# Folding K and V in one strided sum, and dealing the setup steps by weight, in an attention + MoE + FFN kernel

## The chip, the cores and the metric

The kernel runs on one core of a Trainium2 chip. The metric is device time in microseconds (us) of one execution. Three runs of the kernel before took 1839.75, 1842.72 and 1853.4 us; the median is 1842.72 us.

## What is computed

Inputs are q, k, v of shape (8 batches, 8 heads, 576 tokens, 64), a gate, a noise and two expert weight sets, and two FFN weights. Cut to what matters here:

```
k_p = k.reshape(B, H, 72, 8, D).mean(axis=3)      # K and V pooled: 8 tokens become one
v_p = v.reshape(B, H, 72, 8, D).mean(axis=3)
attn = softmax(q @ k_p.T / sqrt(D)) @ v_p          # (8, 8, 576, 64)
x = attn.transpose(0, 2, 1, 3).reshape(4608, 512)
top2 of  x @ w_gate + log1p(exp(x @ w_noise)) * noise   -> 2 of 8 experts per token
out = sum over the two experts of weight * (relu(x @ w1[e]) @ w2[e])
h = out @ w_in;  result = (h * cos(h)) @ w_out
```

The change touches the first stage alone: the pooling of K and V, attention, gating, and the scatter of each token's row into the queues of its two experts.

## The kernel before, in words

**Stages.** Attention with gating takes about the first 290 us, then come the experts (about 290 to 1030 us) and the FFN. The experts start when all rows are scattered: `load_x` reads `xs` back, transposed, by DMA.

**Pairs, units, slots.** Attention works on pairs of batches, `g` = 0 to 3 (called pair 0 to pair 3). A tile is 128 tokens, 64 of each batch of the pair; a pair has R = 9 tiles. A *unit* is two tiles (the last unit of a pair has one), so a pair has 5 units and there are NU = 20, `u` = 0 to 19; `it = u % 5` is the place in the pair. A unit issues its work in the fixed order of the string `ORDER` (line 619): scores of unit u+2 (`S`, on TensorE, with a row maximum on VectorE), transposes of the exponentials of unit u (`T`), the softmax sums of unit u+1 (`N`, on VectorE, and a product on GpSimd, line 399), attention times V (`A`: matmuls into `xp`, a copy on ScalarE, a subtraction on VectorE), exponentials (`E`, ScalarE), transposes of q for unit u+3 (`Q`). Every engine runs its own instructions in the order of this program; the schedule is written out by hand (`manual_schedule`), and the framework only adds waits.

**Setup steps.** Beside the units there is work that belongs to another pair, cut into steps:
- `pooled` (lines 233 to 245): one chunk of K (`pk`, 5 steps) or of V (`pv`, 5 steps) of the next pair, folded on VectorE. A partition holds one window of 8 tokens x 64 for each of two batches, 1024 numbers; the step adds halves three times (512, 256 and 128 numbers; the last addition of K writes its 64 sums twice, side by side).
- `k_tr` (4 steps): three TensorE transposes and two ScalarE copies that put the pooled K into `kbd`, on partitions 0 to 63 and again on 64 to 127.
- `scale_v`, `scale_v2`, `v_tr` x 4, `g_proj1`, `g_proj2`: the scale of V, the seven GpSimd products that lay V out (`vbd`, line 292), its transposes, and the product of V with the gate weights.
- `gating` (10 steps `s1` to `s6` with two empty ones): logits, noise, top 2, ranks of the rows within their expert (`s5` is a group of matmuls, line 520, on what VectorE just wrote).
- `scatter` (9 steps, one per tile): two indirect DMAs each, issued by GpSimd (line 565).
- `prep_steps` for the first expert's weights, in pair 3 only (line 117).

**Slots.** `ORDER` has seven places `G` in a unit, called slots; at each, `go()` (line 621) issues the next steps of the list `fill`: their number over the slots left, rounded up. At the first unit of a pair the list is made: the setup of the next pair, mixed by count (`mix`) with the gating and the scatters of the pair before. In the last pair it is the weights of expert 0 mixed with gating and scatters of pair 2; its own gating follows in three parts in units 18, 19 and behind the loop (`CUTS`).

**Queues.** Loads are issued by the SyncE queue (SP) in program order; a load of K or V waits until its buffer (two of them, named `w1` in the code, `w` in the rows) has been folded. `zero_x` (one DMA) and `zero_y` (18) write zeros to DRAM from the same queue. GpSimd's queue (POOL) carries the softmax product of each unit, the layout of V and all scatters.

Of the kernel before, what the change touches and what calls it, by code (L numbers as in the profile page):

```python
# [34 lines left out]
def tile_attn_moe_ffn(ctx: ExitStack, tc: tile.TileContext, q, k, v, wgate, wnoise, noise,  # L35
# [192 lines left out]
    def setup_steps(g):  # L228
# [4 lines left out]
        def pooled(src, nm, i):  # L233
            def f():
                if i == 0:
                    X[nm + "f"] = src.pop(g).rearrange("p c b e -> p (c b) e")
                    X[nm] = ap_.tile([128, 10, 2 if nm == "ks" else 1, D], F32, name=nm)
                t, o = X[nm + "f"], X[nm]
                n = 64 if nm == "ks" and i == 4 else 128
                t, o = t[0:n, 2 * i:2 * i + 2, :], o[0:n, 2 * i:2 * i + 2, :, :]  # L240
                for w in (256, 128):
                    V.tensor_add(t[:, :, 0:w], t[:, :, 0:w], t[:, :, w:2 * w])  # L242
                dup = [n, 2, 2 if nm == "ks" else 1, D]
                V.tensor_add(o, t[:, :, None, 0:D].to_broadcast(dup), t[:, :, None, D:2 * D].to_broadcast(dup))
# [12 lines left out]
        def k_tr(b, half):
            def f():
                t = tr_half(X["ks"].rearrange("p c s d -> p c (s d)"), b, half).rearrange("p (h n) -> p h n", n=KP)
                for i in range(2):  # L260
                    A.activation(kbd[64 * i:64 * i + 64, b, 4 * half:4 * half + 4, i, :], t[64 * i:64 * i + 64],
                                 AF.Copy, scale=1.0 / 64.0)
            return f

        def scale_v():
            vp = X["vp"].rearrange("p c s d -> p c (s d)")
            m1 = ap_.tile([128, 1], F32, name="vm1")
            V.reduce_max(m1, vp, axis=AX.XY, apply_absolute_value=True)
            mb_ = ap_.tile([128, 128], F32, name="vmb")
            V.tensor_copy(mb_, m1.to_broadcast([128, 128]))  # L270
            X["mb"] = mb_

        def scale_v2():
            mb_, vp = X["mb"], X["vp"].rearrange("p c s d -> p c (s d)")
# [12 lines left out]
            vbd, vbd4 = GS[g]  # L287
            vp4 = vp.rearrange("p (c b) d -> p c b d", b=2)
            for c, o, i0, i1 in ((0, 64, 0, 2), (1, 0, 0, 1), (1, 80, 1, 3), (2, 0, 0, 3), (3, 0, 0, 1), (3, 80, 2, 3),
                                 (3, 144, 1, 2)):  # L290
                n = i1 - i0
                PL.tensor_mul(vbd[:, c, :, o:o + 64 * n].rearrange("p b (i d) -> p b i d", d=D),
                              vp4[:, c, :, None, :].to_broadcast([128, 2, n, D]),
                              rms[:, c, None, i0:i1, None].to_broadcast([128, 2, n, D]))
            V.tensor_scalar(vbd4[:, :, 16:80], vp[:, 8:10, :], s, None, op0=OP.mult)
            VBD[g] = GS[g]

        def v_tr(b, half):
            def f():
                if b == 0 and half == 0:  # L300
                    X["vt"] = ap_.tile([64, 2, S], F32, name="vtt")
                t = tr_half(X["vp"].rearrange("p c s d -> p c (s d)"), b, half)
                A.activation(X["vt"][:, b, 288 * half:288 * half + 288], t, AF.Copy)
            return f

# [311 lines left out]
    CUTS = {3: (0, 6), 4: (6, 8)}  # L617
    left = [0]
    ORDER = "S0 G T0 G T1 S1 E0 T2 N A0 G A1 E1 S2 G A2 Q0 E2 G S3 G A3 Q1 G E3".split()

    def go():
        k_ = -(-len(fill) // left[0])
        left[0] = max(left[0] - 1, 1)
        for f in fill[:k_]:
            f()
        del fill[:k_]

    for u in range(NU):
        g, r, n = UNITS[u]
        it = u % 5  # L630
        if it == 0:
            a = []
            if g + 1 < G:
                pk, kt_, pv, sv = setup_steps(g + 1)
                a = pk + pv[:2]
                for i in range(4):
                    a += kt_[i:i + 1] + pv[i + 2:i + 3]
                a += sv
                if g + 2 < G:
                    a.append(lambda g=g: (load_kv(g + 2, 0), load_kv(g + 2, 1)))  # L640
            if g == G - 1:
                p1, p2 = prep_steps(0, "w1"), prep_steps(0, "w2")
                p1.pop(0)()
                a = p1
            fill += mix(a, late)
            late = []
        if g == G - 1 and it in CUTS:
            r0, r1 = CUTS[it]
            gt = gating(g, r0, r1)
            gt.pop(0)()  # L650
            fill += gt + [scatter(g, r_) for r_ in range(r0, r1)]
            if it == 3:
                p2.pop(0)()
        left[0] = ORDER.count("G") * ((5 if g < G - 1 or it > 2 else 3) - it)
        if g == G - 1 and it == 3:
            left[0] = 6
        for op in ORDER:
            k_ = int(op[1:] or 0)
            if op == "A0":
# [16 lines left out]
                q_tr(u + 3, k_)  # L676
        if u == 2:
            zero_x()
        if 4 <= u <= 12:
            zero_y(2 * u - 8)  # L680
            zero_y(2 * u - 7)
        if it == 4:
            assert not fill
            if g + 2 < G:
                load_q(g + 2)
            if g < G - 1:
                late = gating(g, 0, R)
# [708 lines left out]
```

## Time and profile before

| what | value |
|---|---|
| median of three runs | 1842.72 us (1839.75 to 1853.4) |
| profiled execution, span from first to last instruction | 1814.0 us, 28.7 us below the median; the page gives no time beside the span |
| TensorE busy | 1721.6 us, 95% |
| VectorE, ScalarE, GpSimd busy | 1061.6, 928.8, 423.0 us |
[...]
| chain that ended last | TensorE 87%, VectorE 8%, ScalarE 2%, DMA 1%, GpSimd 1% |

The busy shares are means over very different stages: the FFN and the experts keep TensorE at 90% or more of nearly every slice, the first 315 us do not. So the attention stage has to be read by itself, in stretches of one pair and less. Pair 0 runs to about 97 us, pair 1 to 159, pair 2 to 220, pair 3 to about 282, and the first expert matmul starts at 301.5 us.

### The profile page before, as it was taken

How to read it: one execution, taken by the hardware profiler on the slowest of the kernel's cores; microseconds unless marked ns; L12 is line 12 of the kernel's file. 1: busy time of each engine (PE TensorE's matmuls, PEld its weight loads, DVE VectorE, ACT ScalarE, POOL GpSimd, SP SyncE). 2: the span in 40 equal slices, each digit the busy share in tenths (PEclk: the TensorE clock that was granted, in tenths of full speed). 3: DMA queues.
4: the chain of work that ended last, by engine and by line, in shares of the span. 5: the costliest groups of instructions: out<-in, count | busy, mean ns of one | idle time of the engine just before them, and what ended most of it. 6: DMA issues, size and time to landing. Idle time of an engine off the chain costs nothing.

```text
span 1814.0 us, 28287 instructions
## 1 busy us (share of the span) xinstructions
PE 1721.6 (95%) x11160; PEld 1017.4 (56%) x11160; DVE 1061.6 (59%) x2016; ACT 928.8 (51%) x1843; POOL 423.0 (23%) x457
## 2 busy tenths in 40 slices
PE   5977975999999999999999998999999999999999
PEld 3655652464445544464445545666666666666665
DVE  7787684644666484527674144666656566565633
ACT  4766851323233243323333235777777777767765
POOL 1225663000100000001110013524434243333222
PEclk8988986999999999999999999999999999999999
DMA  9978446456453738474744443313223031222100
GB/s 277 316 249 324 152 163 186 143 177 198 128 169 116 186 99 259 128 213 109 224 123 112 180 145 122 88 35 76 65 70 78 34 88 50 73 61 63 42 24 24
DMA packets 233206, 243.48 MB, mean 134 GB/s; under 512 B 154352, under 2 KB 167664, under 8 KB 232432
## 3 DMA queue, kind: packets, MB, share of 16 engines
q1 hardware_dynamic: 210544, 183.97, 35.0%
q0 software_dynamic: 11520, 37.76, 6.3%
q10 hardware_dynamic: 11008, 19.93, 3.1%
q8 instruction: 88, 1.44, 0.3%
q14 instruction: 46, 0.38, 0.1%
HBM read 127.06 MB, written 78.12 MB: 113 GB/s over the span
## 4 chain that ended last, share of the span: by engine, by line
PE 87%; DVE 8%; ACT 2%; issue 1%; DMA 1%; POOL 1%; SPq 0%; ACTq 0%; POOLq 0%; DVEq 0%
PE ph L1289 20%; PE ph L807 20%; PE py L832 19%; PE py L1252 15%; PE xp L450 3%; PE pt L1252 3%; PE sc L369 2%; DVE w L242 1%; PE py L847 1%; PE tr L416 1%; PE tr L353 1%; PE sc L254 1%; DVE amw L137 1%; DVE w L154 1%; ACT w L153 0%
## 5 line engine op out<-in xcount | busy, mean ns | idle before, releaser
L807 PE MATMUL ph<-xt,w 128*128 128x512 f16 (+1 forms) x2304 | 410.9, 336 | 11.1 <-DMA xt<-xs 11.1
L1289 PE MATMUL ph<-w,ht 128*128 128x512 f16 x1728 | 413.1, 379 | 1.0 <-POOL ht L1279 1.0
L832 PE MATMUL py<-w,ht 128*128 128x512 f16 x1728 | 384.4, 379 | 0.1
L807 PEld LDWEIGHTS <-w 128*128 128x128 f16 x2304 | 214.9, 98 | 198.0 <-issue 16.8
L1279 POOL TENSOR_TENSOR ht<-ty,ht 128x512 f16<-128x512 f32 x144 | 183.7, 1281 | 479.5 <-ACT ht L1278 323.8
L832 PEld LDWEIGHTS <-ht 128*128 128x128 f16 x1728 | 168.6, 98 | 199.1 <-DVE ht L820 0.6
L820 DVE SCALAR_TENSOR_TENSOR ht<-ph,ht 128x512 f16<-128x512 f32 (+2 forms) x192 | 109.9, 574 | 270.3 <-ACT ht L819 270.1
L1289 PEld LDWEIGHTS <-ht 128*128 128x128 f16 x1728 | 169.1, 98 | 152.8 <-POOL ht L1279 1.5
L1252 PEld LDWEIGHTS <-st 128*128 128x128 f16 x1872 | 183.1, 98 | 54.9 <-issue 4.0
L819 ACT ACTIVATE ht<-ph 128x512 f16<-128x512 f32 (+2 forms) x192 | 96.3, 502 | 184.4 <-PE ph L807 157.7
L835 ACT ACTIVATE yt<-py,ysc 128x512 f32<-128x512 f32 x72 | 49.4, 686 | 227.4 <-PE py L832 226.7
L1252 PE MATMUL py<-xt,st 128*128 128x256 f16 x1040 | 139.3, 273 | 3.5 <-ACT ht L1342 3.5
L1264 DVE SCALAR_TENSOR_TENSOR ty<-ty,k,ht 128x512 f32<-128x512 f32 x108 | 94.0, 871 | 83.1 <-ACT ty L1258 83.1
L1273 DVE SCALAR_TENSOR_TENSOR ty<-ty,ht 128x512 f32<-128x512 f32 x108 | 74.7, 692 | 108.8 <-ACT ty L1270 108.8
L1252 PEld LDWEIGHTS <-w 128*128 128x128 f16 x1152 | 112.7, 98 | 39.1 <-issue 3.8
L1269 ACT ACTIVATE ty<-ty,k 128x512 f32<-128x512 f32 x144 | 102.8, 714 | 22.9 <-DVE ty L1264 22.8
L1258 ACT ACTIVATE ty<-ht,k 128x512 f32<-128x512 f32 x108 | 77.4, 717 | 67.3 <-DVE ht L1343 34.1
L1252 PE MATMUL py<-w,st 128*128 128x256 f16 x832 | 111.7, 273 | 0.0
L1278 ACT ACTIVATE ht<-ty 128x512 f16<-128x512 f32 x144 | 89.5, 622 | 34.9 <-DVE ty L1273 34.3
L898 POOL TENSOR_TENSOR tm<-yg 128x512 f32<-128x512 f32 x32 | 33.8, 1057 | 302.7 <-DVE x L908 151.9
L1036 POOL DMA_INDIRECT yg<-yb,yidx x72 | 73.1, 1015 | 113.3 <-DMA yb<-yt 93.5
L1270 ACT ACTIVATE ty<-ty 128x512 f32<-128x512 f32 x144 | 90.7, 630 | 4.6
(249 smaller groups left out, 2095.2 us busy)
## 6 DMA issues: line engine op xcount, KB each, us to landing
yb<-yt ACTq DMA_DIRECT2D x72, 256.0 KB, 3.2
st<-in_moe_w_dram SPq DMA_DIRECT2D x8, 2048.0 KB, 13.5
yg<-in_moe_w_in_dram SPq DMA_DIRECT2D x32, 512.0 KB, 4.9
yg<-in_moe_w_out_dram SPq DMA_DIRECT2D x32, 512.0 KB, 4.4
yb<-zt SPq DMA_DIRECT2D x18, 768.0 KB, 19.8
st<-in_moe_w_dram SPq DMA_DIRECT2D x8, 1536.0 KB, 7.7
w<-in_k_dram SPq DMA_DIRECT2D x16, 512.0 KB, 5.8
w<-in_v_dram SPq DMA_DIRECT2D x16, 512.0 KB, 8.8
```

Source lines behind the costliest of these rows:

```text
L807: PE.matmul(ps[:, 0:n], w[:, a_, k_, 128 * f:128 * f + 128], xt[:, 4 * b_ + k_, 0:n], start=(i == 0), stop=(i == 11))
L819: A.activation(t[:, 0], p, AF.Relu)
L820: V.scalar_tensor_tensor(t[:, 1], p, 0.0, t[:, 0], op0=OP.max, op1=OP.subtract)
L832: PE.matmul(ps[0:m], ht[:, a_, f, 128 * t:128 * t + m], w[:, b_, f, :], start=(i == 0), stop=(i == 23))
L1252: PE.matmul(o, FW["in"][4 * a_ + 2 * sa + k_][:, f:f + 128], x[:, :, sb, k_, :], start=(start and h == 0 and k_ == 0 and j == 0), stop=(k_ ...
L1258: A.activation(y, h, AF.Identity, bias=CB["k4", c][:, 0:1])
L1264: V.scalar_tensor_tensor(y, y, CB["k4", c][:, 0:1], h, op0=OP.subtract, op1=OP.subtract)
L1269: A.activation(y, y, AF.Sin, scale=CB["k4", c][:, 1:2])
L1270: A.activation(y, y, AF.Square, scale=math.sqrt(2.0 * CC))
L1278: A.activation(g[:, 2 * b, :], y, AF.Copy)
L1279: PL.tensor_sub(g[:, 2 * b + 1, :], y, g[:, 2 * b, :])
L1289: PE.matmul(ps, g[:, 2 * b + a_, 256 * h + 128 * tt:256 * h + 128 * tt + 128], FW["out"][b_][:, k_, :], start=(q_ == 0 and b < 2 and h == ...
```

## The change

Four things, all in the attention stage:
1. `pooled` is one `reduce_sum` over the 8 tokens of a window: 1024 numbers in, 128 out, the 8 numbers of one sum 64 apart (256 bytes). K's sums are stored once.
2. Because K's sums are stored once, its transposes give 64 partitions, and both copies into `kbd` read partitions 0 to 63.
3. The steps carry weights. A pair's steps fall into two lists: units 0 to 2 take K (and the gating of the pair before), units 3 and 4 take V (and the scatters of the pair before, which had followed the gating). `blend` merges two lists by weight; `go()` issues steps while half the next weight still fits into the mean weight per slot.
4. K and V of the pair after next are loaded right behind their own folds, no longer behind all of the setup; `zero_y` comes two units later.

```diff
         def pooled(src, nm, i):
...
-                for w in (256, 128):
-                    V.tensor_add(t[:, :, 0:w], t[:, :, 0:w], t[:, :, w:2 * w])
-                dup = [n, 2, 2 if nm == "ks" else 1, D]
-                V.tensor_add(o, t[:, :, None, 0:D].to_broadcast(dup), t[:, :, None, D:2 * D].to_broadcast(dup))
+                t = X[nm + "f"][0:n, i]
+                V.reduce_sum(X[nm][0:n, 2 * i:2 * i + 2, :], t.rearrange("p b (r d) -> p b d r", d=D), axis=AX.X)
...
-                    A.activation(kbd[64 * i:64 * i + 64, b, 4 * half:4 * half + 4, i, :], t[64 * i:64 * i + 64],
+                    A.activation(kbd[64 * i:64 * i + 64, b, 4 * half:4 * half + 4, i, :], t,
...
+    def gate_steps(gt):
+        return cost(gt, 0.3, 0.6, 0.6, 1.4, 1.5, *[0.3] * (len(gt) - 9), 0.5, 0.3, 1.0, 0.7)
     def go():
-        k_ = -(-len(fill) // left[0])
-        left[0] = max(left[0] - 1, 1)
-        for f in fill[:k_]:
-            f()
-        del fill[:k_]
+        goal = sum(c for c, _ in fill) / max(left[0], 1)
+        last = left[0] <= 1
+        left[0] -= 1
+        done = 0.0
+        while fill and (last or done + fill[0][0] / 2 <= goal):
+            done += fill[0][0]
+            fill.pop(0)[1]()
...
+        if it == 0 and g + 1 < G:
+            pk, kt_, pv, sv = setup_steps(g + 1)
+            a = cost(pk, 1.2)
+            if g + 2 < G:
+                a.append((0.0, lambda g=g: load_kv(g + 2, 0)))
+            fill += blend(a + cost(kt_, 0.4), gate_steps(late))
+            late = cost([scatter(g - 1, r_) for r_ in range(R)] if g else [], 0.3)
+            left[0] = 3 * NG
+        elif it == 3 and g + 1 < G:
+            a = cost(pv, 1.2)
+            if g + 2 < G:
+                a.append((0.0, lambda g=g: load_kv(g + 2, 1)))
+            fill += blend(a + cost(sv, 1.2, 0.0, 2.5, 0.4), late)
+            left[0] = 2 * NG
+        elif it == 0:
+            p1, p2 = prep_steps(0, "w1"), prep_steps(0, "w2")
+            p1.pop(0)()
+            fill += blend(cost(p1, 1.2, 1.2, 1.2, 1.2, 1.5, 1.3),
+                          gate_steps(late) + cost([scatter(g - 1, r_) for r_ in range(R)], 0.3))
+            left[0] = 3 * NG
+        elif g == G - 1 and it in CUTS:
...
+            fill += gate_steps(gt) + cost([scatter(g, r_) for r_ in range(r0, r1)], 0.3)
+            left[0] = NG
...
-        if 4 <= u <= 12:
-            zero_y(2 * u - 8)
-            zero_y(2 * u - 7)
+        if 6 <= u <= 14:
+            zero_y(2 * u - 12)
+            zero_y(2 * u - 11)
```

Carrying out the two rules by hand gives the steps of each slot (a bar between slots, "-" an empty one; K0 is the first fold of K, am and sp the maxima and splits of expert 0's weights, sc a scatter):

```
pair 1 before, unit 0  K0 s1 | K1 s2 | K2 s3 | K3 s4a | K4 V0 | s4b V1 | nop kt0
               unit 1  s5 V2 | kt1 nop | V3 | s5b | kt2 | s6 | V4
               unit 2  kt3 | sc0 | scv | sc1 | nop | sc2 | scv2
               unit 3  vt0 | sc3 | vt1 | sc4 | vt2 | sc5 | vt3
               unit 4  gp1 | sc6 | nop | sc7 | gp2 | sc8 | load
pair 1 after,  unit 0  K0 | s1 s2 | s3 | K1 | - | - | s4a
               unit 1  K2 | - | - | s4b | K3 | nop | K4
               unit 2  s5 | nop | s5b | loadK kt0 | kt1 kt2 | s6 | kt3
               unit 3  V0 | sc0 V1 | sc1 V2 | sc2 V3 | sc3 V4 | sc4 loadV | scv
               unit 4  sc5 nop | - | - | scv2 | sc6 vt0 sc7 vt1 | vt2 vt3 sc8 | gp1 nop gp2
pair 0 after: the five K folds in unit 1 slot 3 to unit 2 slot 4, the five V folds in slots 1 to 5 of unit 3
pair 3 before, unit 15 am0 s1 | s2 s3 | am1 s4a | s4b am2 | nop s5 | am3 nop | s5b scl
               unit 16 s6 | sc0 | sp0 | sc1 | sc2 | sp1 | sc3
               unit 17 sc4 | sp2 | sc5 | sc6 | sp3 | sc7 | sc8
pair 3 after,  unit 15 am0 | s1 s2 | s3 | am1 | s4a | am2 | s4b
               unit 16 am3 | scl | nop s5 | nop | sp0 | s5b | s6
               unit 17 sp1 | sc0 sc1 | sp2 | sc2 sc3 sc4 | sc5 | sp3 | sc6 sc7 sc8
```

## Rows read from the trace of the kernel before

**Rows 1.** Page, slices of 45 us: busy tenths of TensorE.
```profile
PE   5977975999999999999999998999999999999999
```
**Rows 2.** Busy time by stretch (columns: stretch, length, engines' busy us, PEclk, DMA, GB/s).
```profile
62.00:97.00 35.00, 34.83 (x384) 25.27 (x385) 23.24 (x71) 29.95 (x112) 10.92 (x11) 1.00 1.05 318
97.00:120.00 23.00, 13.30 (x124) 8.95 (x124) 21.79 (x62) 10.71 (x40) 2.12 (x1) 0.77 0.95 349
120.00:135.00 15.00, 14.64 (x162) 10.51 (x162) 12.30 (x36) 12.03 (x46) 4.74 (x6) 0.90 0.29 89
135.00:159.00 24.00, 23.36 (x249) 16.91 (x246) 13.55 (x46) 20.33 (x76) 21.37 (x36) 1.00 1.03 359
220.00:267.00 47.00, 34.77 (x348) 24.45 (x348) 37.74 (x113) 28.00 (x98) 30.19 (x47) 0.85 0.44 158
```
**Rows 3.** Waits, 97 to 135 us (who for whom: us, times, longest).
```profile
PE tr L520 <- DVE g_ohb L514: 6.1, 1, 6.1
```
**Rows 4.** Groups by line, VectorE and ScalarE, 97 to 135 us (busy us, mean ns).
```profile
L242 DVE TENSOR_TENSOR w<-w 128x512 f32<-128x512 f32 (+3 forms) x20 | 13.9, 696 | 0.3
L244 DVE TENSOR_TENSOR ks<-w 128x256 f32<-128x256 f32 (+1 forms) x5 | 2.1, 424 | 0.2
L244 DVE TENSOR_TENSOR vp<-w 128x128 f32<-128x128 f32 x5 | 1.5, 292 | 0.2
L261 ACT ACTIVATE kbd<-sc 64x288 f32<-64x288 f32 x8 | 3.2, 406 | 0.2 <-PE sc L254 0.2
```
**Rows 5.** Groups by line and shape, VectorE reductions, 0 to 400 us.
```profile
L137 DVE TENSOR_REDUCE amw<-st 128x1 f32<-128x1024 f32 x16 | 19.2, 1208 | 0.0
...
L923 DVE TENSOR_REDUCE fm<-yg 128x1 f32<-128x512 f32 x10 | 6.8, 675 | 0.0
...
L533 DVE TENSOR_REDUCE g_osum<-g_ohb 128x8 f32<-128x72 bf16 x3 | 0.8, 272 | 0.0
```
**Rows 6.** The same view, 267 to 301 us: line 533 on 48 numbers.
```profile
L533 DVE TENSOR_REDUCE g_osum<-g_ohb 128x8 f32<-128x48 bf16 x1 | 0.2, 232 | 0.0
```
**Rows 7.** Timeline of VectorE (start us, duration us, instruction).
```profile
29.82 3.05 DVE L242 TENSOR_TENSOR w<-w 128x512 f32<-128x512 f32 x2
...
97.09 1.14 DVE L242 TENSOR_TENSOR w<-w 128x512 f32<-128x512 f32 x2
...
103.17 3.02 DVE L242 TENSOR_TENSOR w<-w 128x512 f32<-128x512 f32 x2
...
226.99 1.21 DVE L137 TENSOR_REDUCE amw<-st 128x1 f32<-128x1024 f32 x1
```
**Rows 8.** Timeline of GpSimd: softmax products beside them, and scatters of pairs 2, 3.
```profile
103.06 2.12 POOL L399 TENSOR_TENSOR ex<-ex,rc 128x1152 f32<-128x1152 f32 x1 [6.93 <-DVE rc L398]
...
226.87 2.11 POOL L399 TENSOR_TENSOR ex<-ex,rc 128x1152 f32<-128x1152 f32 x1 [1.50 <-PE sc L369]
...
237.79 1.01 POOL L565 DMA_INDIRECT xs<-xr,idx  x1 [8.78 <-DVE mb L112]
...
288.82 0.96 POOL L565 DMA_INDIRECT xs<-xr,idx  x1 [0.22 <-issue]
```
**Rows 9.** Chain that ended last, in order of time: start, us, what.
```profile
8.81 0.61 DVE w L242
10.32 0.61 DVE w L242
...
290.08 4.47 DMA xs<-xr,idx
```
**Rows 10.** VectorE's softmax sums of units 16 and 17 (timeline).
```profile
240.53 1.04 DVE L394 TENSOR_REDUCE sm<-ex 128x12 f32<-128x864 f32 x1
...
252.89 1.04 DVE L394 TENSOR_REDUCE sm<-ex 128x12 f32<-128x864 f32 x1
```
**Rows 11.** SyncE's queue: load of K of pair 2.
```profile
56.69 8.40 SPq L77 DMA_DIRECT2D w<-in_k_dram  x5
```
**Rows 12.** DMA issues 60 to 100 us: KB each, median us to landing.
```profile
w<-in_k_dram SPq DMA_DIRECT2D x2, 512.0 KB, 14.8
```

More of the change, by code (lines that the diff above doesn't have):

```diff
@@ L235, in f @@
                 if i == 0:
-                    X[nm + "f"] = src.pop(g).rearrange("p c b e -> p (c b) e")
-                    X[nm] = ap_.tile([128, 10, 2 if nm == "ks" else 1, D], F32, name=nm)
-                t, o = X[nm + "f"], X[nm]
+                    X[nm + "f"] = src.pop(g)
+                    X[nm] = ap_.tile([128, 10, D], F32, name=nm)
                 n = 64 if nm == "ks" and i == 4 else 128
-                t, o = t[0:n, 2 * i:2 * i + 2, :], o[0:n, 2 * i:2 * i + 2, :, :]
-                for w in (256, 128):
-                    V.tensor_add(t[:, :, 0:w], t[:, :, 0:w], t[:, :, w:2 * w])
-                dup = [n, 2, 2 if nm == "ks" else 1, D]
-                V.tensor_add(o, t[:, :, None, 0:D].to_broadcast(dup), t[:, :, None, D:2 * D].to_broadcast(dup))
+                t = X[nm + "f"][0:n, i]
+                V.reduce_sum(X[nm][0:n, 2 * i:2 * i + 2, :], t.rearrange("p b (r d) -> p b d r", d=D), axis=AX.X)
             return f
@@ L265, in scale_v @@
         def scale_v():
-            vp = X["vp"].rearrange("p c s d -> p c (s d)")
+            vp = X["vp"]
             m1 = ap_.tile([128, 1], F32, name="vm1")
@@ L301, in f @@
                     X["vt"] = ap_.tile([64, 2, S], F32, name="vtt")
-                t = tr_half(X["vp"].rearrange("p c s d -> p c (s d)"), b, half)
+                t = tr_half(X["vp"], b, half)
                 A.activation(X["vt"][:, b, 288 * half:288 * half + 288], t, AF.Copy)
@@ L619, in tile_attn_moe_ffn, with cost, blend @@
     ORDER = "S0 G T0 G T1 S1 E0 T2 N A0 G A1 E1 S2 G A2 Q0 E2 G S3 G A3 Q1 G E3".split()
-    def go():
-        k_ = -(-len(fill) // left[0])
-        left[0] = max(left[0] - 1, 1)
-        for f in fill[:k_]:
-            f()
-        del fill[:k_]
+    NG = ORDER.count("G")
+    def cost(fs, *w):
+        return [(w[min(i, len(w) - 1)], f) for i, f in enumerate(fs)]
+    def blend(a, b):
+        sa, sb = sum(c for c, _ in a) + 1e-9, sum(c for c, _ in b) + 1e-9
+        out, i, j, ca, cb = [], 0, 0, 0.0, 0.0
+        while i < len(a) or j < len(b):
+            if j >= len(b) or (i < len(a) and ca * sb <= cb * sa):
+                ca += a[i][0]
+                out.append(a[i])
+                i += 1
+            else:
+                cb += b[j][0]
+                out.append(b[j])
+                j += 1
+        return out
+    def gate_steps(gt):
+        return cost(gt, 0.3, 0.6, 0.6, 1.4, 1.5, *[0.3] * (len(gt) - 9), 0.5, 0.3, 1.0, 0.7)
+    def go():
+        goal = sum(c for c, _ in fill) / max(left[0], 1)
[5 more added lines that the diff above has]
+            fill.pop(0)[1]()
     for u in range(NU):
@@ L630, in tile_attn_moe_ffn @@
         it = u % 5
[L631 to L647, printed above, removed]
+        if it == 0 and g + 1 < G:
[7 more added lines that the diff above has]
+        elif it == 3 and g + 1 < G:
+            assert not fill
+            a = cost(pv, 1.2)
[10 more added lines that the diff above has]
+        elif g == G - 1 and it in CUTS:
             r0, r1 = CUTS[it]
@@ L688, in tile_attn_moe_ffn @@
                 late.pop(0)()
-                late += [scatter(g, r_) for r_ in range(R)]
     tabs = const.tile([1, 3, OVT], I32, name="tabs")
```

13 lines of the change are left out of this document (4 added, 9 removed).

## The prediction

> **What bounds the kernel now.** The page first: TensorE is busy in nine tenths or more of nearly every slice of 45 us, but in six of the first seven it is not [rows 1]. So I read that part by stretch. From 62 to 97 us TensorE works 34.83 of 35.00 us at full clock and VectorE idles 12 us: TensorE is the bound there. From 97 to 120 us, the opening of pair 1, VectorE works 21.79 of 23.00 us and TensorE 13.30, at a mean granted clock of 0.77. From 135 to 159 us TensorE is the bound again and VectorE idles 10.4 us [rows 2]. The waits name the place: TensorE stands 6.1 us before the rank matmuls of `s5`, for what VectorE writes in `s4` [rows 3]; VectorE is late because all ten folds fall into this stretch, 13.9 + 2.1 + 1.5 = 17.5 us of its work [rows 4]. Pair 2 opens the same way. So a pair loses about 10 us to uneven dealing, twice; the limit of any gain is some 20 us of 1842.72. After attention nothing changes: experts and FFN keep their time.
>
> The profiled execution has a span of 1814.0 us and the page knows no time beside it; the median run is 28.7 us longer. I add the changes to the span and carry the 28.7 along.
>
> **The fold.** Now a fold of K takes 1.51 us from start to start (10.32 - 8.81) [rows 9]; one of V ends with 292 ns in place of 424 [rows 4], so 1.38. A fold that meets the GpSimd product of a softmax is stretched: its first two additions took 3.02 us in place of 1.14, while the product ran [rows 7, 8]. The new step is a reduction of 1024 numbers, 64 apart, which no row shows. From below: line 137 reduces 1024 adjacent numbers in 1.208 us. A step of two numbers costs nothing visible: 512 of them take 0.675 us, about what half of line 137 plus its fixed part gives. But line 533 reads its 72 numbers eight apart (16 bytes) and takes 272 ns [rows 5], and 232 ns for 48 [rows 6]: 1.67 ns each, against 1.04 in line 137 and 923 (1208 - 675 over 512). By that slope the fold takes 0.152 + 1024 x 0.00167 = 1.86 us. I take it, since a step of 256 bytes is nearer to one of 16 bytes than to none. Upper end: that, stretched by 0.6 us on average, which is a third of the 1.9 us that the product added to the additions: 2.5 us. I don't take the stretch, since the reduction of line 137 ran through a product undisturbed, 1.21 us from 226.99 while the product ran from 226.87 to 228.98 [rows 7, 8]. Consecutive instructions overlap by some 0.08 us, so a fold occupies 1.78 us (ends: 1.13 and 2.4).
>
> [...]
>
> **The sum.**
> 1. Start: the five K folds of pair 0 lie on the chain [rows 9]: 5 x (1.78 - 1.51) = **+1.3** (ends -2, +4.5). Its V folds: 5 x 0.4 more, less the 1.9 us of the one that collided at 29.82 [rows 7]: **0** (-2, +3).
> 2. Pair 0, unit 0: K's folds leave it, **-1** (0 to -2): TensorE works there almost without a break.
> 3. Units 0 to 2 of pairs 1 and 2 (38 us in pair 1): VectorE has 21.79 + 12.30 = 34.1 us; without ten folds and with five new ones 34.1 - 17.5 + 8.9 = 25.5. TensorE has 13.30 + 14.64 = 27.9, less at full clock. If nothing collided, 28.5 us; with the ratio of the weight stretch of pair 3, where VectorE works 37.74 of 47.00 us and TensorE 34.77 [rows 2], 25.5 x 1.245 = 31.7. I take 31: units 0 and 1 hold more VectorE than TensorE work and unit 2 less. **-7** each.
> 4. Units 3 and 4 of pairs 0, 1, 2: five V folds come into slots 1 to 5 of unit 3. For two units VectorE has 13.55 - 0.7 + 8.9 = 21.8 us against TensorE's 23.36 of 24.00 [rows 2], but unit 3 alone gets about 14 us of it (an estimate: its own 4, 8.9 of folds, 1.1 of `scv`), where a unit at TensorE's pace lasts about 9.2 us (62 to 97 us holds some 3.8 units). Three PSUM buffers each for scores and products let TensorE run ahead by part of a unit. The last three slots hold all four V transposes and both gate products; their ScalarE copies meet a ScalarE that is busy 29.95 of 35.00 us. I take **+2** for each of the three pairs (0 to +5).
> 5. Pair 3: the weights and gating come more evenly, so units 15 and 16 end 4 us earlier (half of TensorE's waits there). But the scatters of pair 2 start in unit 17, not 16, 12.4 us later by the sums of these units [rows 10] if nothing else moved. GpSimd issues two per tile, 1.26 us apart [rows 8], 36 in all, and softmax products of 2.1 us between: 45.4 + 2.1 = 47.5 us from the first. Now it starts at 237.79 and the last issue starts at 290.08 [rows 8, 9], some 5 us of it idle. Starting at 237.8 + 12.4 - 4 = 246.2, it ends at about 293.7 against 291: **+3** (0 to +8).
>
> Without cost, and why: `kbd` gets its second copy from partitions 0 to 63, 406 ns now [rows 4]; a copy across partitions is not shown, I take the same; twice that would be 3.2 us a pair on ScalarE in slots with spare time, 1 us of it seen. The transposes of K get narrower, a gain below 0.5 us. K's last copy sits in the last slot ahead of the scores that need it: under 1 us, within term 3. Scatters of pairs 0 and 1 in units 3 and 4: 18 x 1.26 = 22.7 us of GpSimd with V's layout and two products, about 29 us in 20, so GpSimd is late by a few us, and the product of the next unit waits behind it; now it is as full, 21.37 of 24 us [rows 2], and TensorE is not late. SP: K of pair 2 is issued at 56.69 now [rows 11], and then only when pair 0's unit 2 has folded K, near 78; it lands some 15 us later [rows 12], just ahead of its first fold near 96; `zero_x` and `zero_y` queue behind it, and nothing needs them soon. If K came late, VectorE would stand once, for 2 or 3 us.
>
> Sum: +1.3 + 0 - 1 - 14 + 6 + 3 = -4.7. **Span 1809, time 1838 us**: a gain that a measurement can hardly tell, since less than 1% (18 us) is not told from no change.
>
> **Rivals.**
> - *Fold at the rate of adjacent numbers*, 1.21 us (1.13 occupied), as line 137. For it: line 923; against it: line 533. Start -4, pair 0 -1 + 1, units 0 to 2 at TensorE's 28.5 us, -9.5 each, units 3 and 4 of pairs 1 and 2 +0.5 each, pair 3 +3: -19, **1824 us**.
> - *The fold is the bound, and it is slower*: 2.5 us. Place: the open slots of units 0, 1 and 3. VectorE then has 34.1 - 17.5 + 12 = 28.6 us in units 0 to 2, 35.6 with the ratio above, -2.4 each; unit 3 holds 17 us in place of some 10, +6 in each pair; start +7.5; pair 0 unit 1 +1; pair 3 +3: -4.8 + 18 + 11.5 = +25, **1867 us**. It turns from gain to loss where a fold takes about 2 us. For it: 40 folds now stand whole in the queue; against it: the slope of line 533. [...]
> - *GpSimd bounds the end*: units 15 and 16 gain nothing, so the scatters end 7 to 8 us later, and the bunches at the ends of units 3 and 4 cost their upper ends: -4.7 + 4 + 6 = +5, **1848 us**. For it: GpSimd's issues follow each other without a break to 291 us.
>
> **Numbers.** Forecast 0.46 (its own range 1829 to 1848), first rival 0.30, second 0.12, third 0.12. The range 1817 to 1856 leaves out the lower tail of the first rival and most of the second. Faster by over 1% (below 1824): half of the first rival and a little, 0.17. Slower by over 1% (above 1861): most of the second, 0.10. Within: 0.73.
>
> **What would show it.** In the trace after: the mean of the one reduction in place of lines 242 and 244 (1.8 to 1.95 us; 1.2 is the first rival, 2.4 the second), also under GpSimd's products; TensorE's wait for `s4` below 2 us; pair 1 from about 96 to 151 us with the clock near 1; a wait of TensorE in unit 3 of each pair; first scatter of pair 2 near 245 us and a start of the experts 3 us later in relation to unit 15. Wrong would make it above all the fold's price, then a VectorE that is late at unit 3 by more than the PSUM buffers take up.

## The result: slower by 1.4%, and the profile after

The changed kernel takes 1867.86 us (median of four runs, 1866.85 to 1872.22), the kernel before beside it 1844.24: a ratio of 1.0139, 95% interval 1.0101 to 1.0178. I had forecast 1838 and given slower by over 1% one chance in ten.

The page of the changed kernel: its profiled execution took 1866.85 us, 1.75 more than its span.

```profile
span 1865.1 us, 28210 instructions
...
PE 1735.2 (93%) x11160; PEld 1022.5 (55%) x11160; DVE 1074.8 (58%) x1936; ACT 927.3 (50%) x1843; POOL 423.2 (23%) x457
...
PE   5887774599999999999999999999999999999999
```

Against [rows 1] the gap of TensorE is a slice longer; the first expert matmul starts at 352.99 us, and from there to the end both kernels take the same, 1512.1 and 1512.5 us. All of the difference lies in attention.

**One trap first.** The trace that I predicted from cannot be set against this one as it stands. The kernel before takes 1836 to 1853 us in some sets of runs (chips 0, 2 and 15) and 1814 to 1818 in others (chips 5 and 6); all runs of one set are on one chip. The chip of the first trace is not known, but its span of 1814.0 us and its times up to pass 14 (passes are explained below) fit the second kind alone: `gate_first_again`, the same kernel up to there on chip 6, reaches that pass at 214.3 us, the trace at 213.9, `before_again` on chip 2 at 227.2. So I take the 28.7 us, which I had carried along as time outside the span, to be this difference of chips. The ratio is the same on both kinds (below), so the loss is read on the second kind, and two experiments there stand for the changed kernel, which did not run there itself: one shares its pairs 0 to 2 (`pair3_count`), one all but the place of the zero writes (`zero_early`). On one chip of the first kind the loss up to pass 15 is 12.8 us (243.3 in `before_tail`, which is the kernel before up to there, 256.1 in `after_again`), on the second 16.2.

**Where the time goes.** I count by VectorE's softmax sums; "pass u" is the sum issued in the loop's turn of unit u, as in [rows 10]. It stands behind the second slot of its unit, so the first two V folds of units 3, 8 and 13 (3.8 us) fall into the row above the one that has term 4's forecast. Times in us between them:

| stretch | before | changed | difference | forecast |
|---|---|---|---|---|
| start to the sum ahead of the loop | 28.1 | 30.3 | +2.2 | +1.3 |
| pair 0, that sum to pass 3 | 55.1 | 54.3 | -0.8 | -1 |
| pair 0, pass 3 to 5 | 18.2 | 26.5 | +8.3 | +2 |
| pair 1, pass 5 to 6 | 20.2 | 12.3 | -7.9 | |
| pair 1, pass 6 to 8 | 19.7 | 26.4 | +6.7 | together with the line above -7 |
| pair 1, pass 8 to 10 | 21.6 | 26.4 | +4.8 | +2 |
| pair 2, pass 10 to 11 | 20.2 | 12.3 | -7.9 | |
| pair 2, pass 11 to 13 | 20.8 | 26.3 | +5.5 | together with the line above -7 |
| pair 2, pass 13 to 15 | 21.4 | 26.5 | +5.1 | +2 |
| pair 3, pass 15 to the first expert matmul | 76.4 | 87.5 | +11.1 | +3 |

The last line is from `zero_early`, the others from `pair3_count`. Before rounding they add up to +27.3; the spans of `zero_early` and of the kernel before differ by 1841.5 - 1814.0 = 27.5.

Busy time by pass, pair 1 of the kernel before, from pass 5 to pass 10 (columns as in [rows 2]):

```profile
101.30:121.50 20.20, 11.72 (x103) 7.95 (x99) 18.32 (x53) 9.19 (x35) 2.12 (x1) 0.70 0.91 331
121.50:132.90 11.40, 11.04 (x125) 7.79 (x123) 9.94 (x32) 8.50 (x29) 4.40 (x5) 0.93 0.13 49
132.90:141.20 8.30, 8.30 (x90) 5.92 (x89) 6.81 (x25) 6.71 (x27) 5.81 (x9) 1.00 0.93 306
141.20:153.10 11.90, 11.73 (x127) 8.66 (x128) 4.42 (x16) 10.07 (x38) 10.63 (x21) 1.00 1.05 348
153.10:162.80 9.70, 8.54 (x97) 6.09 (x95) 7.66 (x23) 8.02 (x38) 8.64 (x12) 1.00 1.03 404
```

The same five passes with the changed dealing (`pair3_count`):

```profile
111.00:123.30 12.30, 10.70 (x119) 7.35 (x117) 11.92 (x27) 8.90 (x38) 2.12 (x1) 1.00 0.66 192
123.30:135.60 12.30, 8.27 (x92) 5.65 (x89) 10.65 (x27) 6.41 (x27) 2.12 (x1) 0.77 0.12 35
135.60:149.70 14.10, 14.10 (x129) 9.58 (x130) 9.58 (x25) 10.29 (x35) 4.39 (x5) 0.83 0.85 289
149.70:160.20 10.50, 6.51 (x71) 4.75 (x69) 10.33 (x22) 5.43 (x22) 7.86 (x15) 0.87 0.37 115
160.20:176.10 15.90, 14.91 (x130) 10.16 (x128) 8.90 (x25) 10.66 (x42) 14.07 (x25) 0.87 1.02 372
```

Read the third column (TensorE) against the fifth (VectorE). Before, one pass is VectorE's (18.32 of 20.20) and in the next three TensorE works almost without a break. After, the passes change hands: VectorE 11.92 of 12.30 and 10.33 of 10.50 where folds stand, TensorE 14.10 of 14.10 and 14.91 of 15.90 where the transposes and products stand, which now follow behind all folds.

What that costs shows in whole pairs, pair 0 and pair 1, each before and after:

```profile
28.10:101.30 73.20, 63.87 (x606) 44.77 (x608) 52.72 (x144) 50.43 (x188) 18.56 (x20) 0.88 1.04 309
30.30:111.00 80.70, 64.85 (x601) 44.95 (x602) 53.38 (x114) 50.22 (x182) 18.52 (x20) 0.87 0.73 216
101.30:162.80 61.50, 51.34 (x530) 36.42 (x528) 47.14 (x142) 42.49 (x160) 31.59 (x46) 0.89 0.82 290
111.00:176.10 65.10, 54.49 (x528) 37.48 (x526) 51.39 (x121) 41.70 (x158) 30.55 (x46) 0.87 0.64 215
```

In pair 0 TensorE stands longer, 15.9 us in place of 9.3, for nearly as much work. In pair 1 it stands as long as before, 10.6 us in place of 10.2, but as many matmuls keep it busy for 54.5 us in place of 51.3. Both show at the same places. At the end of a run of folds VectorE is late with the row maxima, ScalarE with the exponentials, and TensorE stands for about 3 us (`pair3_count`, pair 1; there is such a wait at the end of both runs of folds of that pair and of the V folds of pair 0, of 3.1, 2.9 and 3.0 us in the changed kernel):

```profile
128.66 1.88 DVE L240 TENSOR_REDUCE ks<-w 128x128 f32<-128x1024 f32 x1
130.94 0.95 ACT L379 ACTIVATE ex<-sc,mx 128x72 f32<-128x72 f32 x4 [3.16 <-DVE mx L366]
132.33 0.48 PE L411 MATMUL tr<-idf,ex 128*128 128x128 f32 x1 [3.14 <-ACT et L417]
```

At the end of each of the two waits of pair 1, and while the steps that were held up run, TensorE's granted clock is at 0.51 and 0.50 of full speed (second and third row). In the kernel before there is one such stretch in the pair, at 0.50, and TensorE stands in nearly half of it (first row):

```profile
110.00:123.00 13.00, 6.92 (x42) 4.47 (x42) 11.36 (x36) 4.98 (x19) 0.00 (x0) 0.50 0.72 245
132.30:140.40 8.10, 8.07 (x55) 5.25 (x57) 5.43 (x17) 3.68 (x17) 2.69 (x3) 0.51 0.78 235
157.70:164.10 6.40, 4.57 (x33) 3.19 (x34) 4.86 (x16) 4.50 (x21) 5.29 (x11) 0.50 0.84 258
```

The price can be read from 24 matmuls of line 445 at either level:

```profile
135.95 3.29 PE L445 MATMUL xp<-vbd,et 128*64 128x144 f32 x24
147.48 1.82 PE L445 MATMUL xp<-vbd,et 128*64 128x144 f32 x24
```

At that ratio the 5.7 us more of work at the lower level (8.07 + 4.57 - 6.92) cost some 2.6 us, an estimate, of the 3.6 us that pair 1 loses. No experiment holds the clock by itself, so this part rests on the traces.

In the changed kernel itself the opening wait for `s4` is gone, 0.6 us in place of the 6.1 of [rows 3] (waits, 97 to 150 us):

```profile
PE tr L515 <- DVE g_ohb L509: 0.6, 1, 0.6
```

and the folds (groups by line, to 353 us) answer to [rows 4]: 1.89 to 1.92 us each.

```profile
L240 DVE TENSOR_REDUCE vp<-w 128x128 f32<-128x1024 f32 x20 | 38.1, 1917 | 0.0
L240 DVE TENSOR_REDUCE ks<-w 128x128 f32<-128x1024 f32 (+1 forms) x20 | 37.5, 1891 | 0.0
L256 ACT ACTIVATE kbd<-sc 64x288 f32<-64x288 f32 x32 | 12.9, 402 | 16.0 <-PE sc L249 15.6
```

### The profile page after: what moved, and what is told of

Same layout as the page of the kernel before. It is cut to its first block, busy times and chain, and to the rows that moved or that the text cites. A ratio compares the mean times of both kernels' runs of the same rounds, so it can differ in the third digit from the quotient of the medians.

```text
span 1865.1 us, 28210 instructions
## 1 busy us (share of the span) xinstructions
PE 1735.2 (93%) x11160; PEld 1022.5 (55%) x11160; DVE 1074.8 (58%) x1936; ACT 927.3 (50%) x1843; POOL 423.2 (23%) x457
## 4 chain that ended last, share of the span: by engine, by line
PE 75%; DVE 3%; ACT 1%; DMA 1%; issue 0%; POOL 0%; ACTq 0%; DVEq 0%; POOLq 0%; SPq 0%
PE ph L1312 20%; PE ph L830 19%; PE py L855 18%; PE py L1275 14%; PE pt L1275 2%; PE py L870 1%; DMA yg<-yb,yidx 0%; DVE w L154 0%; DMA xt<-xs 0%; POOL yg L1059 0%; ACT w L153 0%; DVE amw L137 0%; DVE ht L843 0%; DVE ty L1287 0%; DVE x L1074 0%
## 5 line engine op out<-in xcount | busy, mean ns | idle before, releaser
L1287 DVE SCALAR_TENSOR_TENSOR ty<-ty,k,ht 128x512 f32<-128x512 f32 x108 | 94.1, 872 | 81.9 <-ACT ty L1281 81.5
L1301 ACT ACTIVATE ht<-ty 128x512 f16<-128x512 f32 x144 | 89.5, 622 | 34.9 <-DVE ty L1296 34.3
L445 PE MATMUL xp<-vbd,et 128*64 128x144 f32 (+3 forms) x864 | 82.3, 332 | 14.8 <-ACT et L417 10.1
```

The source lines that it names most:

```text
L445: PE.matmul(xp[64 * b:64 * b + 64, c0:c0 + n], lhs[:, 64 * b:64 * b + 64], rhs, start=(c == cs[0][0]), stop=(c == cs[-1][0]), skip_group_c ...
L1287: V.scalar_tensor_tensor(y, y, CB["k4", c][:, 0:1], h, op0=OP.subtract, op1=OP.subtract)
L1301: A.activation(g[:, 2 * b, :], y, AF.Copy)
```

## The experiments

Ratios are to the kernel before in the same set of runs, with 95% intervals.

**The trace, again.** The kernel before, unchanged, on a chip of the first kind.

> The kernel before, unchanged, to settle against which trace the changed one has to be read. The profiled execution that I predicted from had a span of 1814.0 us, the timed runs 1839.75 to 1853.4; in the changed kernel the span is only 1.75 us under the time. Theory 1 (that one execution was an unusually quick one, and a normal one loses some 25 us somewhere in attention): span 1838 to 1850, first expert matmul near 326 us in place of 301.5. Theory 2 (28.7 us lie outside the span, as the prediction assumed): span again 1814, first expert matmul at 301 to 302 us. Theory 3 (a slower clock all over): attention as long as before, and the experts and the FFN 25 us longer.

Ratio 0.9991 (0.9968 to 1.0014), span 1849.7, first expert matmul at 337.8: the span lies in theory 1's range, the matmul 12 us behind it, and theories 2 and 3 fall; the later sets point to the chip, not to an unusual execution.

**The fold alone, from both sides.** `old_fold` is the changed kernel with the three additions back, `new_fold` the kernel before with the one reduction.

```
-  V.reduce_sum(X[nm][0:n, 2 * i:2 * i + 2, :], t.rearrange("p b (r d) -> p b d r", d=D), axis=AX.X)
+  for w in (256, 128):
+      V.tensor_add(t[:, :, 0:w], t[:, :, 0:w], t[:, :, w:2 * w])
+  V.tensor_add(o, ...)
```

> The changed kernel with the old fold: three additions, K's sums stored twice; the weights, lists and loads stay changed. Theory A (the loss is in the dealing; the fold costs little): 1862 to 1872 us, no more than 5 us from the changed kernel's 1868. Theory B (the fold as one whole reduction of 1.9 us is what costs): 1840 to 1850 us, as the kernel before.

> The kernel before with the new fold alone (one reduction, K stored once), dealt by count as before. Theory A (the dealing costs): 1842 to 1852 us; 40 folds that are each 0.4 us longer, most of them in the opening units of pairs 1 and 2, where VectorE is the bound, are worth 40 x 0.4 = 16 us at the very most, and some 4 to 6 us if the old additions no longer collide with GpSimd. Theory B (the fold costs): 1860 us or more.

`old_fold` 1.0120 (1.0087 to 1.0153), 1867.18 us against 1867.86 with the new fold; `new_fold` 1.0001 (0.9978 to 1.0024). Either way the fold makes no difference that these runs can tell: the loss is in the dealing.

**V's weights.** `cost(sv, 1.2, 0.0, 2.5, 0.4)` became 1.0, 0, 1.0, four times 0.8, 1.2, 0, 1.2.

> The changed kernel with other weights for the V steps alone (1.0 for both scale steps, 0.8 for each V transpose, 1.2 for each gate product, in place of 1.2, 2.5, 0.4, 0.4), so that the transposes and products fill unit 4 slot by slot and no longer stand bunched in its last three. In the trace of the changed kernel units 9 to 10 and 14 to 15 take 22 to 24 us from softmax sum to softmax sum where the kernel before takes 10 to 11. Theory A1 (the bunch makes that): both fall to some 12 us and the time to 1845 us (23 us less). Theory A2 (something else withholds TensorE's results there, whatever is dealt): 1862 to 1870 us, with the same long stretch at the same place.

1.0098 (1.0063 to 1.0132), 1863.87 us: 4 us better than the changed kernel and in A2's range, A1 falls. Pair 1, pass 8 to 10, went from 34.3 to 31.1 us only; on this kind of chip the kernel before takes 32.8 us there itself (`before_again`).

**One list, and pair 3 by count** (kernel before at 1815.94).

```
 one_list       - two lists (K + gating | V + scatters), 3 * NG and 2 * NG slots
                + one list K, kt, V, sv blended with gating + scatters, 5 * NG slots
 pair3_count    - blend by weight in pair 3
                + mix(p1, late + scatters), one step counted as one
 zero_early     - zero_y in units 6 to 14      + four after each of units 0 to 4
```

> The changed kernel with one list per pair over all five units in place of two stretches: K folds, K transposes, V folds, V's scale, transposes and products in this order, blended by weight with the gating and scatters of the pair before; the weights of the kernel called spread. So V's chain (scale, transposes, gate products) starts one unit earlier and the scatters follow the gating as in the kernel before. Theory A2 (the second stretch costs: V's chain of TensorE and ScalarE steps, each waiting for the one before, meets the scatters with nothing else to cover it): units 3 and 4 of pairs 1 and 2 back to some 25 us from spread's 31, pair 0 back to 75 us from 82, total 1840 to 1850 us. Theory W (dealing by weight itself costs, since folds in the units where TensorE is the bound hold up the row maxima): as spread, 1860 to 1868 us.

> The changed kernel with the steps of pair 3 alone dealt by count as in the kernel before (scatters of pair 2 start in its second unit again). From the softmax sum of unit 15 to the first expert matmul the changed kernel takes 99.0 us, a normal execution of the kernel before 92 to 94. Theory T (later scatters cost the tail 5 us, as GpSimd's issues bound the end): 1861 to 1864 us. Theory A (the tail is not the place): 1866 to 1870 us.

> Both of the last two edits in one kernel: one list per pair by weight, pair 3 by count. If A2 and T both hold it keeps the gain of the opening units (7 us in each of pairs 1 and 2) without the losses: 1830 to 1838 us, faster than the kernel before. If dealing by weight costs of itself: 1855 us or more.

> The changed kernel with the 18 DMAs that write zeros issued in pair 0 (four after each unit) in place of units 6 to 14, so that none runs beside the scatters of pairs 0 and 1. Theory D (traffic beside the scatters is what holds the engines up for 5 us and more at the ends of pairs 1 and 2): the long stretches of 24 and 22 us fall to some 15 as in pair 0, total 1850 to 1856 us. Otherwise no change, 1864 to 1870 us.

`one_list` 1.0127 (1.0110 to 1.0143): A2 falls as I put it. Passes 8 to 10 came back to 22.9 us, but passes 5 to 8 took 42.7, because V's scale now follows the last V fold at once and TensorE, in order, stands for it (waits of TensorE, 133.2 to 148.6 us):

```profile
PE tr L271 <- DVE vmb L265: 5.9, 1, 5.9
```

`pair3_count` 1.0090 (1.0073 to 1.0107), `one_list_p3` 1.0075 (1.0058 to 1.0092), `zero_early` 1.0140 (1.0123 to 1.0157). So dealing pair 3 by count returns 8.5 us (1833.59 against 1842.05 in `zero_early`), more than theory T's 4 to 7. `one_list_p3`, expected faster than the kernel before, is slower: with one list in place of two and pair 3 by count 0.75% stays. Theory D is not tested: its stretches of 24 and 22 us belong to the first kind of chip, and on this one that at the end of pair 1 is 16.0 us with the writes in either place. What `zero_early` does show is that the place of the writes costs nothing up to pass 15 (241.78 us, 241.26 in `pair3_count`), and that the changed dealing loses the same 1.4% on this kind of chip. The first scatters, `pair3_count`:

```profile
241.26 1.04 DVE L389 TENSOR_REDUCE sm<-ex 128x12 f32<-128x864 f32 x1
...
253.94 1.01 POOL L560 DMA_INDIRECT xs<-xr,idx  x1 [8.75 <-DVE mb L112]
...
319.05 2.29 PE L839 MATMUL ph<-xt,w 128*128 128x512 f16 x5 [11.33 <-DMA xt<-xs]
```

and `zero_early`:

```profile
241.78 1.04 DVE L389 TENSOR_REDUCE sm<-ex 128x12 f32<-128x864 f32 x1
...
269.99 1.01 POOL L560 DMA_INDIRECT xs<-xr,idx  x1 [6.43 <-DVE idx L537]
...
329.29 2.29 PE L830 MATMUL ph<-xt,w 128*128 128x512 f16 x5 [14.56 <-DMA xt<-xs]
```

From pass 15's sum the first scatter comes 12.7 us later in the one and 28.2 in the other. From there the 36 issues with their products take GpSimd's queue in both, and the experts start 65.1 and 59.3 us after the first, 11.6 and 10.2 us after the start of the last issue (307.45, 319.06; before 11.4, after 290.08). The edit moves all steps of pair 3; that the scatters are what counts is read from these times.

**The order inside the stretches.**

> The changed kernel again, to set its trace against the kernel before on one chip: the kernel before took 1838 to 1853 us in some sets of runs and 1814 to 1818 us in the last. If this set is like the last one (kernel before near 1816 us): 1838 to 1844 us, pair 0 some 7 us longer than before, pairs 1 and 2 some 3 us each, from the softmax sum of unit 16 to the first expert matmul some 11 us. If it is like the earlier ones: 1866 to 1872 us.

> The changed kernel with another order and other weights inside its two stretches: the two K transposes that need only the first three folds come right behind these, the other two at the end (0.8 each in place of 0.4), and V's transposes, scale and products the same way (0.8, 1.0 and 1.2). Pair 3 as changed. Theory O (in each stretch the folds come first and the transposes last, so the units are bound by VectorE, 10.3 to 11.9 us of 10.5 to 12.3, and by TensorE, 14.1 of 14.1 and 14.9 of 15.9, in turn, and the sum of the maxima is longer than the mean): units 2 and 4 shorten by 3 us each and the others stay, some 5 us in each of pairs 0, 1 and 2, ratio to the kernel before 1.005 to 1.008. Theory N (the order does not matter; the units are bound by the sum of waits of all): 1.012 to 1.016.

`after_again` 1.0130 (1.0098 to 1.0162); its expectation counts the sums one further, as do those of the next group. `interleaved` 1.0227 (1.0189 to 1.0264): 15 us slower than the changed kernel, outside theory O's range and theory N's too. Pair 0, in which no scatter runs, took 80.8 us against 81.5; the late pass got shorter (12.4 for 16.2) and the one before it longer (13.5 for 10.4). Why the rest got slower I did not find.

**The rule for the slots.** `carry` lets the debt of a slot go over to the next:

```
-  goal = sum(c for c, _ in fill) / max(left[0], 1)     # this slot alone
-  while fill and (last or done + fill[0][0] / 2 <= goal):
+  goal = plan[0] * (plan[1] - left[0]) / plan[1]       # all slots so far
+  while fill and (left[0] <= 0 or plan[2] + fill[0][0] / 2 <= goal):
```

`carry_p3` has pair 3 by count beside it, `mended_pl` the interleaved order too, `mended` also three softmax products on VectorE.

> The changed kernel with one edit: the slots' debt is carried over, so a step is issued when the weights issued so far fall half a step behind an even share (stretches, order and weights as changed). Theory L (the changed rule issues heavy steps late: in pair 0 no K fold before slot 4 of unit 1, then all five in eight slots): pair 0 from the first softmax sum to that of unit 6 in 73 to 76 us in place of 80 to 81; total 6 to 10 us less, ratio 1.008 to 1.011. Theory S (the two stretches cost, not the rule): pair 0 still 79 to 81 us, ratio 1.012 to 1.015.

> The same with pair 3 dealt by count as in the kernel before. Theory L with T: the two gains add up, ratio 1.002 to 1.006. Theory S: as the changed kernel with pair 3 by count, 1.008 to 1.010.

> The last one with the interleaved order and its weights as well: the kernel called mended, but with all softmax products on GpSimd again. In mended pair 0 took 73.4 us and the three products on VectorE left GpSimd 18 scatters in a row, behind which TensorE's results came late. Without that: ratio 0.998 to 1.005, pair 0 again 73 to 74 us; if the order has no part in it, as carry_p3.

> The interleaved order, with the slots' debt carried over (a step is issued when the weights issued so far fall behind an even share; in the changed rule a step of 1.2 waits until the mean weight per remaining slot reaches 0.6, which leaves the first slots of a stretch empty and fills the last), pair 3 dealt by count as before, and the softmax products of the last four units on VectorE in place of GpSimd. Theory O with T (GpSimd's issues bound the end; each product of 2.1 us taken off it is worth up to that): ratio 0.992 to 0.999. If the order and the carry bring nothing: 1.005 to 1.010.

`carry` 1.0088 (1.0068 to 1.0109), `carry_p3` 1.0051 (1.0032 to 1.0071), `mended_pl` 1.0054 (1.0036 to 1.0073), `mended` 1.0140 (1.0109 to 1.0170). Theory L holds: pair 0 took 76.0 us with the carry alone, and the two gains add up. `mended`, expected faster than the kernel before, missed by far; without the products on VectorE (`mended_pl`) it loses 0.5% (last section). What `carry_p3` still loses, 0.5%, no run returned; 2 us of it are the start with the new fold. With the interleaved order as well pair 0 took 74.0, as before (73.2), TensorE's granted clock in its late pass is 1.00 in place of 0.85, and 19 matmuls of that pass come earlier: the late pass of pair 0, with the carry alone and with both (`carry_p3`, `mended_pl`):

```profile
91.90:106.50 14.60, 13.69 (x108) 9.18 (x110) 7.82 (x23) 8.78 (x32) 5.53 (x8) 0.85 1.03 269
```

```profile
94.70:104.20 9.50, 9.39 (x89) 6.41 (x89) 6.90 (x22) 7.02 (x25) 5.52 (x8) 1.00 0.98 297
```

The total does not gain from that: in these two traces the order returns 2.3 us in pair 0 and costs 4.1 in pairs 1 and 2; which of its steps does that I did not separate.

**GpSimd's products.** `before_tail`: the kernel before with three softmax products of pair 3 on VectorE.

> The kernel before with one edit: the softmax products of units 16, 17 and 18 on VectorE (that of 19 is there already). Theory T (from the first scatter of pair 2 on GpSimd's issues follow each other without a break, so its queue bounds the start of the experts, and each product of 2.1 us taken from it brings that forward): 3 to 6 us less, ratio 0.9967 to 0.9983. If the attention's last unit bounds the end instead: no change or up to 2 us more, since VectorE gets 1.5 us per unit.

1.0098 (1.0066 to 1.0130), 19 us slower where theory T had 3 to 6 us less: as a rule for the kernel before it falls here (last section).

**Scatters sooner, in the kernel before.** `fill += mix(a[:3], late[:10]) + mix(a[3:], late[10:])` in pair 3.

> The kernel before with one edit: in pair 3 the ten gating steps of pair 2 are mixed with the first three steps of the weights, ahead of the scatters and the other weight steps, so that the first scatter comes about two slots sooner (the last slot of unit 15 in place of the second of unit 16). Theory T (from the first scatter on GpSimd bounds the start of the experts): 2 to 4 us less, ratio 0.9975 to 0.999. If something else bounds it: 0.999 to 1.002.

> The kernel before with gating ahead in pair 3, once more with five rounds. Theory T: 0.9975 to 0.9995, with an interval below 1. If it was chance: 0.9995 to 1.0015.

> The same with the one-reduction fold and K stored once. If the fold costs nothing beside it either: within 0.001 of gate_first_again. If the longer fold shows where VectorE is the bound: 0.001 to 0.003 above it.

0.9985 (0.9969 to 1.0000), then, on a chip of the second kind, 1.0001 (0.9992 to 1.0011): no gain, and no test of T, since the edit did not move what it meant to. In `gate_first_again` the first scatter starts at 237.38 in place of 237.79, waiting for the index, and later GpSimd waits for pair 3's own indices:

```profile
237.38 1.01 POOL L565 DMA_INDIRECT xs<-xr,idx  x1 [7.87 <-DVE idx L542]
...
271.62 0.96 POOL L565 DMA_INDIRECT xs<-xr,idx  x1 [2.84 <-DVE idx L542]
```

With the new fold beside it 1.0016 (1.0007 to 1.0026): on this chip the times scatter less, and the fold costs some 2.5 us (1818.53 against 1816.02), most of it the start (30.2 for 28.1). No version that I ran beats the kernel before.

## Why the prediction was wrong, step by step

The step that failed is the dealing, terms 3 to 5. Terms 3 and 4 let TensorE run through the stretches with folds, ahead by its PSUM buffers and at full clock; it stood at their ends (3.1 and 2.9 us in pair 1) and worked 12.6 us of that pair at the lower clock level, in place of 6.9. Term 5 let pair 3 end 3 us later, and it ended 11.1 us later.

**The fold: right.** 1.86 us forecast from the slope of line 533, 1.89 to 1.92 measured. Line 137's 1.21 is not what the trace shows, so the first rival was out. The second, a fold of 2.5 us, gave 1867, the right number for a wrong reason: no fold took longer than 1.97 us, and `old_fold` loses nearly as much. Term 1 was +2.2 for +1.3.

**Term 3 (opening units, -7 each): failed, -1.2 and -2.4.** The wait at `s4` went as said, and pass 5 to 6 alone gained 7.9 us. But the term took 25.5 us of VectorE work and a ratio, and TensorE's work as "less at full clock". In passes 5 to 8 of pair 1 VectorE works 32.2 us, 3.8 of them V folds, and TensorE 33.1, with the wait and the lower clock shown above; the sign "with the clock near 1" failed (0.87 over the pair). The K transposes, left at "a gain below 0.5 us" (their matmuls took 274 ns before and 273 after, medians) and "under 1 us" for the last copy, are in it too. They had been spread over units 0 to 2; now, at 0.4 each and behind all folds, they stand in four slots at the end of unit 2. ScalarE there, in `pair3_count`:

```profile
142.15 1.65 ACT L256 ACTIVATE kbd<-sc 64x288 f32<-64x288 f32 x4
143.82 0.21 ACT L547 ACTIVATE g_w<-g_w 128x9 f32<-128x9 f32 x1
```

`g_w`, on which VectorE waits 1.84 us, stands behind four of their copies. That pass takes 14.1 us for 8.3, of which the first 4.8 are at the lower clock. No run separates the transposes from the clock: `interleaved` moves two of the four forward, among other steps, and passes 5 to 8 take 42.3 us there against 38.8 in `after_again`.

**Term 4 (units 3 and 4, +2 per pair): right in kind, mis-sized: +8.3, +4.8, +5.1.** It saw that VectorE gets about 14 us of work in unit 3 and let TensorE run ahead by part of a unit; the closing "a VectorE that is late at unit 3 by more than the PSUM buffers take up" is what came. Its rows also named the bunch of V transposes and products and priced it by ScalarE's busy share. These steps are a chain, transpose, copy, product, copy, transpose, copy; TensorE is busy in it nearly throughout (5.12 of 5.30 us from 101.5), and the row maximum behind it lets VectorE wait 4.75 us (the changed kernel, end of unit 4 in pair 0):

```profile
101.54 0.91 PE L249 MATMUL sc<-idf,vp 128*64 128x128 f32 x6
102.55 2.17 PE L308 MATMUL tr<-vtt,wgn 64*16 64x144 f32 x16
105.39 0.79 PE L320 MATMUL tr<-idf,gt 16*128 16x16 f32 x10
```

```profile
106.86 0.46 DVE L366 TENSOR_REDUCE mx<-sc 128x4 f32<-128x288 f32 x1 [4.75 <-PE sc L364]
```

So the same bunching has TensorE wait for VectorE in one pass and VectorE for TensorE in the next. My own table of slots showed empty slots early in a stretch and full ones at its end, and I drew nothing from it. A step of 1.2 waits until the mean per remaining slot is 0.6; that is what `carry` undid (0.4 to 0.5% of the time).

**Term 5 (tail, +3): the third rival's mechanism, sized too small: +11.1.** I subtracted 4 us for faster units 15 and 16 and let the 5 us of GpSimd's idle time absorb the rest. The units got slower (pass 15 to 17 in 32.2 us for 27.8), and the first scatter came 28.2 us after pass 15's sum in place of 12.7 (237.79 in [rows 8] less 225.1). From it to the experts `zero_early` takes 59.3 us and the kernel before 63.7: 15.5 less 4.4 is the measured 11.1. The 4.4 are mainly a wait of 2.24 us and a product of 2.11, which GpSimd had between its scatters in the kernel before; the term counts one product there where the trace has two, at 242.31 and 255.99, and takes the second for idle time:

```profile
242.31 2.11 POOL L399 TENSOR_TENSOR ex<-ex,rc 128x1152 f32<-128x1152 f32 x1 [2.24 <-PE xp L450]
```

In the changed kernel itself the first scatter starts at 281.21:

```profile
281.21 1.01 POOL L560 DMA_INDIRECT xs<-xr,idx  x1 [6.07 <-DVE idx L537]
```

The third rival gave 1848 from an end 7 to 8 us later.

**What was costed at nothing** came out so: K of pair 2 was issued at 75.8 and nobody waited for it, and the place of the zero writes had no part up to pass 15 (`zero_early`). One reading of the page was off without effect: in [rows 1] five of the first seven slices are below nine tenths, not six.

In sum: terms 3 and 4 carry 22.8 us of the 32 between -4.7 and +27.3 (their border is blurred by the two V folds), term 5 8.1.

## What to carry to other kernels

When steps are dealt anew, list for each slot what every engine gets before and after, not the engine that the change relieves: work taken off VectorE's crowded unit was worth 8 us there, and the folds bunched ahead of the transposes and products cost 5 to 8 us in each later stretch. Where the other engine stands at the end of such a bunch, look at its clock behind the wait. A rule that compares a step with the mean per remaining slot issues heavy steps late; carry the debt. And before a trace is set against timed runs, look whether its own execution's time is among them.

## What the runs showed of the hardware

**Traces on two kinds of chip.** On the chips where the kernel before takes 1844 us, engines wait for TensorE although its matmuls are recorded as done, in stretches in which GpSimd issues scatters one behind the other. In the changed kernel matmuls of line 445 start at 158.82 and take 2.82 us, yet ScalarE's copy of their result waits; `remote` says that the signal has no sender in the profile:

```profile
158.82 2.82 PE L445 MATMUL xp<-vbd,et 128*64 128x144 f32 x24 [2.92 <-ACT et L417]
...
162.95 0.96 POOL L560 DMA_INDIRECT xs<-xr,idx  x1 [0.22 <-issue]
...
165.96 0.66 ACT L448 ACTIVATE xr<-xp 128x256 f16<-128x256 f32 x2 [5.38 <-remote]
```

The copy starts 2 us after the last of ten scatters in a row. In `before_tail` 18 stand in a row, from 256.95 to 279.76, since no product breaks them; TensorE's records come one by one, about 1.4 us apart, and ScalarE waits 11.3 us, until 2.8 us after the last:

```profile
274.07 0.41 PE L353 MATMUL tr<-idf,st 128*64 128x128 f32 x1 [1.03 <-issue]
275.48 0.37 PE L353 MATMUL tr<-idf,st 128*64 128x128 f32 x1 [1.00 <-issue]
```

```profile
282.59 0.38 ACT L453 ACTIVATE xr<-xp 128x256 f16<-128x256 f32 x1 [11.30 <-remote]
```

Pass 16 to 17 takes 29.7 us there and 12.4 in `before_again`, which is most of the 19 us of `before_tail`. `mended` has the same 18 in a row and 26.5 us in that pass, `mended_pl`, with the products back on GpSimd, 12.4. On the chips of 1816 us 32 scatters in a row, in `zero_early`, leave no such wait in the trace (the longest of ScalarE's copies there, 5.2 us, is for matmuls of line 445). What differs between the chips, and whether the recording itself has a part in it, stays open.

**Beside a GpSimd product** of 2.12 us a fold nearly keeps its time (1.97 us, 1.89 in the mean), while an addition of 72 numbers with two inputs takes nine times its own (0.23 us a moment later); the changed kernel:

```profile
61.38 2.12 POOL L394 TENSOR_TENSOR ex<-ex,rc 128x1152 f32<-128x1152 f32 x1 [11.28 <-DVE rc L393]
...
112.41 2.12 POOL L394 TENSOR_TENSOR ex<-ex,rc 128x1152 f32<-128x1152 f32 x1 [8.42 <-ACT xr L448]
```

```profile
61.51 1.97 DVE L240 TENSOR_REDUCE ks<-w 128x128 f32<-128x1024 f32 x1
...
112.57 2.04 DVE L491 TENSOR_TENSOR g_lu<-g_lu,g_u 128x72 f32<-128x72 f32 x1
114.64 0.23 DVE L492 TENSOR_TENSOR g_lu<-g_lu,nz 128x72 f32<-128x72 f32 x1
```

So the collision that the old fold suffered in [rows 7] did not vanish with it; another addition stands there now. The number of inputs alone does not decide it: the addition has two and the fold one, but an instruction of 18 numbers with one input (line 524, at 273.56 us) took 1.55 us beside the product that starts at 272.96, and 0.16 us in pair 0's gating (at 132.97). What else tells it from the fold no run shows.
